# A second bank of inner products in a TensorE-bound mixer kernel: the third product of both mixers as seven half-size products over a VectorE base

## The chip, the cores and the metric

The kernel runs on one core of a Trainium2 chip. The metric is the device time of one execution in microseconds (us). All profiled runs named here are fast, with a mean granted TensorE clock between 0.995 and 1.0 of full speed. Ratios are the mean time of one kernel's fast runs over the mean of the other's from the same rounds, with a 95% interval. They are therefore not quite the ratio of the medians that are quoted next to them.

A profile's span is the time from the first to the last instruction of one execution. It is about 1.8 us shorter than the time of that execution (573.1 against 574.88 us before).

## The reference

```python
def reference(A_x, A_wqkv, A_wo, B_x, B_w1, B_b1, B_w2, B_b2):
    x = A_x                                             # 1 x 2048 x 1024
    h = x + attention(layernorm(x), A_wqkv, A_wo)       # linear attention, cut
    n = layernorm(layernorm(h))
    u = gelu(einsum("bsd,sf->bdf", n, w1) + b1)         # mixer 1: 2048 tokens -> 3584
    y = einsum("bdf,fs->bds", u, w2) + b2               # mixer 2: 3584 -> 2048
    return h + y.transpose(0, 2, 1)
```

The attention block takes the first 235 us and the change does not touch it. The two mixers are matrix products and take the rest.

## The kernel before

Both mixers are built from a seven-product scheme for 2 x 2 blocks (Strassen-Winograd), one "pair" of stationary tiles at a time. `p1` to `p7` are products of 512 columns, with 8 steps of the contraction in mixer 1 and 14 in mixer 2. Their results are combined in banks `A`, `B`, `C` of PSUM, the memory into which this program has TensorE write its results, and the fifth product goes to SBUF, where it keeps its working tiles, as `e`. `evac` is an eviction: it takes a finished result out of its bank.

```python
    def p1: mm(1, A);  ScalarE: B <- A
    def p6: mm(6, B);  ScalarE: C <- B       # both accumulate onto the copied bank
    def p2: mm(2, A);  evac(0, 0, A)
    def p7: mm(7, C);  evac_shared(1, C)     # VectorE: t = C + e, then out
    def p3: mm(3, B);  evac_shared(0, B)     # VectorE: t = B + e, then out
    def p4: mm(4, C);  evac(1, 0, C)
    def asum(m):  # VectorE: stationary operand of products 5, 6, 7, 3 as a sum of tiles
```

Two pairs form a "quad". One product of a quad, `m`, can itself be split by the same scheme: its four sub-blocks of 256 columns and half the contraction become seven inner products `i1` to `i7` instead of eight. A quad holds two pairs, so one product costs 16 matmuls of 512 columns in mixer 1; the seven inner products are 28 matmuls of 256 columns. (28 and 49 in mixer 2.)

```python
    class Inner:                              # a, e share one PSUM bank; b, c the other
        def i1: mm(1, a); ScalarE: b <- a
        def i6: mm(6, b); ScalarE: c <- b
        def i2: mm(2, a); sink(0, 0, a)       # hand the finished part on
        def i5: mm(5, e); ScalarE: es <- e
        def i7: mm(7, c); sink_sum(1, 1, c, es)   # VectorE adds es
        def i3: mm(3, b); sink_sum(0, 1, b, es)
        def i4: mm(4, c); sink(1, 0, c)
```

Between these steps `interleave` puts the matmuls of another product as filler, so that TensorE has work while ScalarE and VectorE hand banks on. Before the change, mixer 1 has the first and the fifth product inner in its six later quads, mixer 2 the fifth in its three later quads:

```python
        def run(self, pend, nxt, ...):        # one quad
            interleave(self.in1, [st.p4 for st in pend])
            nxt = nxt()                       # weights of the next quad
            interleave(self.in5, [st.p6 for st in self.sts])
            pre(5)                            # VectorE sums for the NEXT quad
            for st in self.sts: st.p2()
            pre(6)
            for st in self.sts: st.p7()
            pre(7)
            for st in self.sts: st.p3()
            pre(3)
```

In mixer 2, `out` takes a result through an SBUF tile `ot` (three of them) and writes it out with a DMA; `hr` are tiles of the residual `h`, read back from memory.

Of the kernel before, what the change touches and what calls it, by code (L numbers as in the profile page):

```python
# [8 lines left out]
P = 128  # L9
# [18 lines left out]
def kernel(  # L28
# [171 lines left out]
    class Inner:  # L200
        def __init__(self, sts, m, mov, tag, sink, sink_sum):
            self.nk, self.mov, self.tag = sts[0].nk // 2, mov, tag
            self.sink, self.sink_sum = sink, sink_sum
            L = [st.lhs[m].rearrange("p (k two) f -> p k two f", two=2) for st in sts]
            self.a11, self.a12, self.a21, self.a22 = (L[i][:, :, h, :] for i in range(2) for h in range(2))
            self.lhs = {1: self.a11, 2: self.a12, 4: self.a22}

        def sums(self):
            sm = [pools["is"].tile([P, self.nk, P], FP16, tag=self.tag, bufs=4, name="is")[:] for _ in range(4)]
            nc.vector.tensor_tensor(sm[0], self.a21, self.a22, ALU.add)  # L210
            nc.vector.tensor_tensor(sm[1], sm[0], self.a11, ALU.subtract)
            nc.vector.tensor_tensor(sm[2], self.a11, self.a21, ALU.subtract)
            nc.vector.tensor_tensor(sm[3], self.a12, sm[1], ALU.subtract)
            self.lhs.update({5: sm[0], 6: sm[1], 7: sm[2], 3: sm[3]})
# [23 lines left out]
        def i5(self):  # L238
            self.mm(5, self.e, True)
            self.es = cpool.tile([P, HW], F32, tag="es", name="es")  # L240
            nc.scalar.copy(self.es[:], self.e)

        def i7(self):
            self.mm(7, self.c, False)
            self.sink_sum(1, 1, self.c, self.es[:])

        def i3(self):
            self.mm(3, self.b, False)
            self.sink_sum(0, 1, self.b, self.es[:])
# [5 lines left out]
    class Product7:  # L255
# [9 lines left out]
        def prefetch(self):  # L265
            pass

        def asum(self, m):
            a, b, op = {
                5: (self.a21, self.a22, ALU.add),  # L270
                6: (self.lhs.get(5), self.a11, ALU.subtract),
                7: (self.a11, self.a21, ALU.subtract),
                3: (self.a12, self.lhs.get(6), ALU.subtract),
            }[m]
            t = pools["sa"].tile([P, self.nk, P], FP16, tag="sa", name="sa")[:]
            self.lhs[m] = t
            return nc.vector.tensor_tensor(t, a, b, op)  # L277
# [50 lines left out]
        def p7(self, cut=None):  # L328
            self.mm(7, self.C, False)
# [4 lines left out]
            self.evac_shared(1, self.C)  # L334
# [34 lines left out]
    class Mixer2(Product7):  # L369
        def __init__(self, p):  # L370
            super().__init__(p, w2_tiles[p], NFP, gmov)

        def prefetch(self):
            self.hr = {}
            for sh in range(2):
                for dh in range(2):
                    t = outp.tile([P, CW], BF16, tag=f"hr{self.p % 2}{sh}{dh}", bufs=2 if (sh, dh) == (1, 0) else 1, name="hr")
                    nc.sync.dma_start(t[:], h_dram[2 * self.p + sh][:, dh * CW:(dh + 1) * CW])
                    self.hr[sh, dh] = t

        def out(self, sh, dh, a, b, op):
            i = 2 * self.p + sh
            ot = outp.tile([P, CW], BF16, tag="ot", bufs=3, name="ot")
# [21 lines left out]

    class Quad:
        def __init__(self, sts, mov1, mov5):
            self.sts = sts
            self.mov1, self.mov5 = mov1, mov5
# [19 lines left out]

        def pre(self, m):  # L430
            if m == 5 and self.mov1 is not None:
                self.in1 = Inner(self.sts, 1, self.mov1, "i1", self.sink1, self.sum1)
                self.in1.sums()
            for st in self.sts:
                st.asum(m)
            if m == 5:
                self.in5 = Inner(self.sts, 5, self.mov5, "i5", self.sink5, self.sum5)
                self.in5.sums()

        def prefetch(self):  # L440
            for st in self.sts:
                st.prefetch()

        def run(self, pend, nxt, on_p4=nop, before_p7=nop, on_p7=nop, cut=None):
            nk = self.sts[0].nk

            def interleave(n, fs):
                steps = [(f, k) for f in fs for k in range(nk)]
                t = len(steps)
                cuts = [0, (5 * t + 8) // 16, (9 * t + 8) // 16, (12 * t + 8) // 16, t]  # L450

                def fill(q):
                    part = steps[cuts[q]:cuts[q + 1]]
                    for f in fs:
                        ks = [k for g, k in part if g is f]
                        if ks:
                            f(ks)

                for f in (n.i1, 0, n.i6, n.i2, 1, n.i5, n.i7, 2, n.i3, 3, n.i4):
                    fill(f) if isinstance(f, int) else f()  # L460

            if self.mov1 is not None:
                for st in self.sts:
                    st.begin()
                interleave(self.in1, [st.p4 for st in pend])
            else:
                for st in self.sts:
                    st.p1()
                for st in pend:
                    st.p4()  # L470
            on_p4()
            nxt = nxt()
            for st in self.sts:
                st.shared_tile()
            interleave(self.in5, [st.p6 for st in self.sts])
            pre = nxt.pre if nxt is not None else (lambda m: None)
            pre(5)
            for st in self.sts:
                st.p2()
            pre(6)  # L480
            before_p7()
            for st in self.sts:
                st.p7(cut if st is self.sts[-1] else None)
            on_p7()
            pre(7)
            for st in self.sts:
                st.p3()
            pre(3)
# [13 lines left out]

    def run_pair(st, pend, nxt, after1=nop, after5=nop, on_p4=nop, before_p7=nop, on_p7=nop):
        st.p1()
        after1()
        if not pend:
            h = st.nk // 2
            st.p5(list(range(st.nk - 1)))
            st.p2(list(range(h)))
            st.p5([st.nk - 1])  # L510
        else:
            for q in pend:
                q.p4()
            on_p4()
            st.p5()
        after5()
        nxt.pre(5)
        st.p6()
        nxt.pre(6)
        st.p2(None if pend else list(range(h, st.nk)))  # L520
        before_p7()
        st.p7()
        on_p7()
        nxt.pre(7)
        st.p3()
        nxt.pre(3)
        return [st]
# [662 lines left out]
    pools["is"] = inner1  # L1190
    hmov.update(moving(hE, hO, hT2, hT3, hT4))
    mov1, sums1 = inner_moving(hE[:, :, 0:CW], NSP, inner1, "hi1")
    mov5, sums5 = inner_moving(hE[:, :, CW:D], NSP, inner1, "hi5")
    NQ1 = NFP // 2

    def next_load1(u):
        def load():
            if u < NQ1:
                load_w1(u, 0)
                load_w1(u, 1)  # L1200
            else:
                load_w2(0, wpool)
        return load

    def quad1(u):
        return Quad([Mixer1(2 * u), Mixer1(2 * u + 1)], mov1, mov5)

    nxt = Mixer1(1)
    pend = run_pair(cur, [], nxt)
    cur, nxt = nxt, quad1(1)  # L1210

    pend = run_pair(cur, pend, nxt, after1=sums1, after5=sums5)
    for u in range(1, NQ1):
        cur = nxt
        pend, nxt = cur.run(pend, lambda: quad1(u + 1) if u + 1 < NQ1 else None, on_p4=next_load1(u + 1))
# [4 lines left out]
    pools["sa"] = ctx.enter_context(tc.tile_pool(name="sapool2", bufs=6, side="right", reuse_waits="tile"))  # L1220
# [4 lines left out]
    pools["is"] = inner2  # L1225
# [4 lines left out]
    cur.asum(5)  # L1230
    for sl in spans:
        nc.vector.tensor_tensor(gT2[:, sl, :], gO[:, sl, CW:D], gE[:, sl, CW:D], ALU.subtract)
    for m in (6, 7, 3):
        cur.asum(m)
# [15 lines left out]
    mov5, sums5 = inner_moving(gE[:, :, CW:D], NFP, inner2, "gi5")  # L1250

    def quad2(u):
        return Quad([Mixer2(2 * u), Mixer2(2 * u + 1)], None, mov5)

    def after_p4(u):
        def act():
# [4 lines left out]
        return act  # L1261

    pend = [cur, Mixer2(1)]
    nxt = quad2(1)
    for st in pend:
        st.prefetch()
        if st is pend[1]:
            for m in (5, 6, 7, 3):
                st.asum(m)
            make_t3()  # L1270
        st.p1()
        st.p5()
        st.p2()
        st.p6()
    sums5()
    nxt.pre(5)
    for st in pend:
        st.p7()
    make_t4()
    nxt.pre(6)  # L1280
    nxt.pre(7)
    for st in pend:
        st.p3()
    nxt.pre(3)
    for u in range(1, NSP // 2):
        cur = nxt
        cur.prefetch()
        last = 2 * u + 2 == NSP
        pend, nxt = cur.run(
            pend, lambda: None if last else quad2(u + 1),  # L1290
            on_p4=after_p4(u), on_p7=make_t4, cut=CW - P if last else None,
        )
# [32 lines left out]
```

## Time and profile before

| | before |
|---|---|
| time, median of 4 runs | 574.91 us (574.85 to 575.26) |
| TensorE (PE) | 566.0 us busy, 99% of the span |
| VectorE (DVE) | 383.8 us, 67% |
| ScalarE (ACT) | 254.7 us, 44% |
| DMA | 41.7% of the 16 engines' time on the main queue |

The page of the profile of before, parts 1 and 4. Part 1 gives busy time, share and number of instructions. Part 4 is the chain of work that ended last, followed back from the end, as shares of the span.

```profile
span 573.1 us, 8081 instructions
...
PE 566.0 (99%) x3061; PEld 287.2 (50%) x3061; DVE 383.8 (67%) x731; ACT 254.7 (44%) x547; POOL 1.8 (0%) x8
...
PE 93%; DVE 3%; DMA 2%; ACT 2%; issue 1%; SPq 0%; ACTq 0%
```

TensorE is busy for the whole span and the chain is TensorE. The busy share does not show small losses at hand-offs, so I also used a finer measure. From the trace's matmul starts, a matmul of 512 columns follows its predecessor after 0.216 us and one of 256 columns after 0.109 us (medians in the mixers). Everything by which a start comes later than this cadence I call *excess*. It is read for every pair of neighbouring matmuls and assigned to the place where it falls. Before the change the excess was 3.04 us in mixer 1 and none in mixer 2 (-0.09).

A quad of mixer 1: the timeline, where each line is start, duration, engine, source line, operation, output <- inputs, and in brackets how long the engine stood idle and what ended it. SPq is the queue from which SyncE issues the DMAs. `...` marks rows left out.

```profile
341.93 1.89 PE L285 MATMUL psA_3760<-hO,wq 128*128 128x512 f16 x8
...
343.42 0.42 DVE L210 TENSOR_TENSOR is<-wq 128x512 f16<-128x512 bf16 x1 [2.16 <-DMA wq<-in_B_w_dram]
343.65 1.89 PE L285 MATMUL psA_3762<-hO,wq 128*128 128x512 f16 x8
...
345.38 1.89 PE L285 MATMUL psC_3856<-hT_2231,sa 128*128 128x512 f16 x8
```

VectorE stood 2.16 us at the head of its queue, waiting for the next quad's weights, and TensorE went on with `p2` and `p7` without a gap (1.89 us of busy time for 8 matmuls, starts 1.72 us apart). Second, the end of the kernel:

```profile
569.47 0.62 DVE L388 SCALAR_TENSOR_TENSOR ot<-psC_5541,b_sb,hr 128x384 bf16<-128x384 f32 x1 [1.52 <-PE psC_5541 L285]
569.65 0.55 PE L285 MATMUL psC_5618<-gs_5626,wq 128*128 128x128 f16 x7
570.25 0.35 DVE L388 SCALAR_TENSOR_TENSOR ot<-psC_5618,b_sb,hr 128x128 bf16<-128x128 f32 x1 [0.16 <-PE psC_5618 L285]
```

The last two evictions follow TensorE directly. From the start of the last matmul to the end of the span it is 3.1 us.

### The profile page before, as it was taken

What the parts mean: (1) busy time and instruction counts of PE and PEld (TensorE: products, weight loads), DVE (VectorE), ACT (ScalarE), POOL (GpSimd) and SP (SyncE); (2) the same over time, 40 slices, a digit from 0 to 9 for tenths busy, and PEclk for the clock granted to TensorE, in tenths of its full rate; (3) what the DMA queues carried; (4) which work ended last, traced back from release to release, by engine and by line L of the source; (5) the groups of instructions that cost most, each with busy time, mean ns of one, the idle gap of its engine ahead of it and who ended that gap; (6) DMA issues with size and microseconds to landing.
All of it is one profiled execution on the core that took longest, in us unless ns stands there. A gap on an engine that the chain in (4) does not pass through costs nothing.

```text
span 573.1 us, 8081 instructions
## 1 busy us (share of the span) xinstructions
PE 566.0 (99%) x3061; PEld 287.2 (50%) x3061; DVE 383.8 (67%) x731; ACT 254.7 (44%) x547; POOL 1.8 (0%) x8
## 2 busy tenths in 40 slices
PE   8999999999999999999999999999999999999997
PEld 3444444455555444446555565564444554544544
DVE  6898887556767879863745727442989558557535
ACT  5657777656667776445445354463110100100100
POOL 1000000000000000000000000000000000000000
PEclk9999999999999999999999999999999999999999
DMA  9934432039536762104041240425971852842001
GB/s 309 352 74 83 85 73 38 19 113 318 104 73 130 184 174 102 55 2 146 1 148 55 93 148 1 148 75 146 233 189 47 218 140 67 218 120 73 19 27 47
DMA packets 97798, 66.59 MB, mean 116 GB/s; under 512 B 32082, under 2 KB 91744, under 8 KB 97760
## 3 DMA queue, kind: packets, MB, share of 16 engines
q1 hardware_dynamic: 97024, 65.42, 41.7%
q10 hardware_dynamic: 672, 0.66, 0.3%
q8 instruction: 24, 0.39, 0.3%
q14 instruction: 14, 0.11, 0.1%
q0 software_dynamic: 64, 0.01, 0.0%
HBM read 50.34 MB, written 8.39 MB: 102 GB/s over the span
## 4 chain that ended last, share of the span: by engine, by line
PE 93%; DVE 3%; DMA 2%; ACT 2%; issue 1%; SPq 0%; ACTq 0%
PE acc_t L964 9%; PE acc_t L1112 9%; PE psB L695 4%; PE psC L695 4%; PE psA L695 4%; PE psE L695 2%; PE nd_ps L1063 1%; DMA xr<-in_A_x_dram 1%; PE psB_4758 L285 1%; PE psC_5500 L285 1%; PE psC_5181 L285 1%; PE psB_5064 L285 1%; PE psC_4858 L285 1%; PE psA_4757 L285 1%; PE psC_4527 L285 1%; PE psB_4550 L285 1%
## 5 line engine op out<-in xcount | busy, mean ns | idle before, releaser
L285 PEld LDWEIGHTS <-sa 128*128 128x128 f16 x716 | 70.0, 98 | 77.3 <-issue 0.7
L285 PEld LDWEIGHTS <-wq 128*128 128x128 bf16 x590 | 57.1, 98 | 61.7 <-issue 1.0
L964 PE MATMUL acc_t<-xnT,wq_sb 128*128 128x512 bf16 x256 | 58.0, 379 | 0.0
L1112 PE MATMUL acc_t<-wo_sb,pqT 128*128 128x512 bf16 x256 | 56.1, 379 | 0.0
L277 DVE TENSOR_TENSOR sa<-wq 128x1024 f16<-128x1024 bf16 (+1 forms) x44 | 36.4, 830 | 6.9 <-DMA wq<-in_B_w_dram 2.8
L1112 PEld LDWEIGHTS <-pqT 128*128 128x128 bf16 x256 | 24.8, 98 | 29.0
L964 PEld LDWEIGHTS <-wq_sb 128*128 128x128 bf16 x256 | 24.5, 98 | 27.4
L166 ACT ACTIVATE e_sb<-acc_t 128x512 bf16<-128x512 f32 x40 | 23.9, 597 | 26.5 <-PE acc_t L964 24.3
L170 DVE TENSOR_SCALAR e_sb<-e_sb 128x512 bf16<-128x512 bf16 x64 | 18.5, 289 | 25.4 <-ACT e_sb L166 24.8
L218 PEld LDWEIGHTS <-is 128*128 128x128 f16 x276 | 26.9, 98 | 14.3 <-issue 3.0
L695 PEld LDWEIGHTS <-xs 128*128 128x128 f16 x208 | 20.0, 98 | 23.3 <-DVE xs L681 1.3
L695 PE MATMUL psA<-wkv,xnT 128*128 128x512 bf16 x104 | 26.7, 379 | 0.0
L1123 DVE BATCH_NORM_STATS2 hst<-acc_t 128x6 f32<-128x512 f32 x32 | 22.1, 693 | 6.7 <-ACT h_bf L1122 6.5
L1110 ACT CAST acc_t<-xr 128x512 f32<-128x512 bf16 x32 | 19.0, 593 | 13.4 <-DVE hst L1123 13.3
L695 PEld LDWEIGHTS <-xnT 128*128 128x128 bf16 x156 | 15.3, 98 | 18.5 <-issue 0.2
L167 ACT ACTIVATE r_sb<-acc_t 128x512 bf16<-128x512 f32 x40 | 23.7, 593 | 0.0
L619 PE MATMUL acc_t<-wkv,xnT 128*128 128x512 bf16 x96 | 21.6, 379 | 0.7 <-ACT xnT L872 0.7
L1084 DVE TENSOR_TENSOR o_sb<-nd_ps,rd 128x384 bf16<-128x384 f32 (+1 forms) x48 | 21.7, 504 | 0.6 <-ACT rd L1079 0.4
L588 DVE BATCH_NORM_STATS2 st<-x_sb 128x6 f32<-128x512 bf16 x32 | 20.5, 681 | 1.6 <-DMA x_sb<-in_A_x_dram 1.6
L277 DVE TENSOR_TENSOR sa<-sa,wq 128x1024 f16<-128x1024 f16 (+1 forms) x22 | 18.3, 831 | 3.9 <-PE psC_4858 L285 2.3
L277 DVE TENSOR_TENSOR sa<-wq,sa 128x1024 f16<-128x1024 bf16 (+1 forms) x22 | 18.3, 831 | 3.7 <-PE psI_5141 L218 1.1
L1122 ACT CAST h_bf<-acc_t 128x512 bf16<-128x512 f32 x32 | 18.4, 575 | 1.0 <-PE acc_t L1112 0.9
(722 smaller groups left out, 979.1 us busy)
## 6 DMA issues: line engine op xcount, KB each, us to landing
wq<-in_B_w_dram SPq DMA_DIRECT2D x14, 1024.0 KB, 7.7
wq<-in_B_w_dram SPq DMA_DIRECT2D x8, 1792.0 KB, 10.0
xr<-in_A_x_dram SPq DMA_DIRECT2D x16, 256.0 KB, 3.1
out_dram<-ot SPq DMA_DIRECT2D x31, 128.0 KB, 1.7
x_sb<-in_A_x_dram SPq DMA_DIRECT2D x15, 256.0 KB, 3.2
wkv<-in_A_wqkv_dram SPq DMA_DIRECT2D x2, 1024.0 KB, 9.5
wq_sb<-in_A_wqkv_dram SPq DMA_DIRECT2D x2, 1024.0 KB, 12.7
wo_sb<-in_A_wo_dram SPq DMA_DIRECT2D x2, 1024.0 KB, 6.4
```

The costliest lines, as they stand in the source:

```text
L166: pin(nc.scalar.activation(e_sb[:], src, ACT.Exp))
L167: pin(nc.scalar.activation(r_sb[:], src, ACT.Relu))
L218: nc.tensor.matmul(ps, lhsT=self.lhs[m][:, k, :], rhs=self.mov[m][:, k, :], start=(start and k == 0), stop=(k == self.nk - 1), skip_group_ ...
L277: return nc.vector.tensor_tensor(t, a, b, op)
L285: nc.tensor.matmul(ps[:, cols], lhsT=lhs[:, k, :], rhs=mv(k)[:, cols], start=(start and k == 0), stop=(k == self.nk - 1), skip_group_check ...
L588: return nc.vector.bn_stats(st[:, c, :], x_sb[:, c * CW:(c + 1) * CW])
L619: mm = nc.tensor.matmul(pp[:, 0:CW], lhsT=xnT[:, kt, i * P:(i + 1) * P], rhs=wkv[:, kt, c * CW:(c + 1) * CW], start=(kt == 0), stop=(kt == ...
L695: pin(nc.tensor.matmul(ps[:], lhsT=lhs[:, k, :], rhs=rhs[:, k, :], start=(start and k == 0), stop=(k == hk2 - 1), skip_group_check=True,))
L964: nc.tensor.matmul(qp[:, 0:SW], lhsT=wq_sb[:, kt, j * P:(j + 1) * P], rhs=xnT[:, kt, u * SW:(u + 1) * SW], start=(kt == 0), stop=(kt == ND ...
L1084: nc.vector.tensor_tensor(o_sb[:, b * JPB * P:(b * JPB + nsl) * P].rearrange("p (s h e) -> p s h e", h=HB, e=DH), blk[:, :, 0:P].rearrange ...
L1112: nc.tensor.matmul(ap_[:, 0:CW], lhsT=pqT[:, j, i * P:(i + 1) * P], rhs=wo_sb[:, j, dc * CW:(dc + 1) * CW], start=(j == 0 and not SEED_RES ...
L1123: nc.vector.bn_stats(st[:, dc, :], ap_[:, 0:CW])
```

## The change

The intent is to spare TensorE more columns. The third product becomes inner in all later quads of both mixers, and the fifth also in the first quads. `B` of the third product can't be a bank that the inner products accumulate on, because the inner results are parts of it; so VectorE builds a base `T = B + e` in SBUF and adds the inner results to it. To make room in SBUF, some sums are written in place and some rings of tiles are smaller. The core of the diff, cut:

```diff
@@ class Inner
         def i5(self):
             self.mm(5, self.e, True)
-            self.es = cpool.tile([P, HW], F32, tag="es", name="es")
-            nc.scalar.copy(self.es[:], self.e)
+            if self.mid is not None:
+                self.mid(self.e)                    # third product: VectorE, into T
+            else:
+                ... as before, in a shared tile
@@ class Product7, asum
-            t = pools["sa"].tile([P, self.nk, P], FP16, tag="sa", name="sa")[:]
+            if m == 3 and self.in_place:            # mixer 2
+                t = self.lhs[6]
+            elif m == 7:
+                t = self.a21.bitcast(FP16)          # over the weights
+            else:
+                t = pools["sa"].tile([P, self.nk, P], FP16, tag="sa", name="sa")[:]
@@ class Mixer2, out
-            ot = outp.tile([P, CW], BF16, tag="ot", bufs=3, name="ot")
+            ot = outp.tile([P, CW], BF16, tag="ot", bufs=2, name="ot")
@@ class Quad
+        def base3(self):                            # T = B + e, once for each pair
+                nc.vector.tensor_tensor(t[:], st.B[:], st.e[:], ALU.add)
+        def mid3(self, e):                          # inner fifth product into both T
+                nc.vector.tensor_tensor(t[:, HW:CW], e, t[:, HW:CW], ALU.add)
+        def sum3(self, m, h, ps, es=None):          # the other inner results
+            nc.vector.tensor_tensor(t[:, c], ps, t[:, c], ALU.add)
+            if (m, h) in ((0, 1), (1, 0)):
+                self.sts[m].evac(0, 1, t)
@@ Quad.run
+            self.pre(6)                             # own sums, not the next quad's
+            self.pre(7)
             interleave(self.in5, [st.p6 for st in self.sts])
-            pre(5); p2; pre(6); p7; pre(7); p3; pre(3)      (shortened)
+            self.base3()
+            self.pre(3)
+            self.each("p2")
+            interleave(self.in3, self.p7s(), self.nk)
+            self.tail(nxt)                          # prefetch, then nxt.pre(5)
```

Not shown: a new routine `first` for the first quads, the residual tiles `hr` in one ring of four, and one dummy matmul that seeds a bank.

## The prediction

> **What bounds the kernel now.** TensorE. The profile's first part has PE busy 566.0 of 573.1 us (99%), granted clock 1.0; the chain of waits is 93% PE. From the trace's matmul starts, a 512-column matmul issues every 0.216 us and a 256-column one every 0.109 us[...]. Over both mixers (230 us to the end) everything beyond this cadence sums to about 3 us, 1.4 of it in the first 6 us of mixer 1. VectorE is 67% busy, ScalarE 44%. So only fewer PE columns can help, and any new wait shows in full.
>
> **What PE is spared.** One product of a quad costs 16 (mixer 1) or 28 (mixer 2) matmuls of 512, as seven inner products 28 or 49 of 256: 3.46 -> 3.05 us and 6.05 -> 5.34 us. Seven such replacements in mixer 1 (third product in six quads, fifth in the first) and four in mixer 2 save 7 x 0.40 + 4 x 0.71 = 5.7 us; one added seeding matmul costs 0.2. The reordered first quad should hide about 1 us of mixer 1's start-up waits. With no new waits: about 568.5 us.
>
> **What it adds.** VectorE per steady quad: four inner sums (0.42 us each in mixer 1, 0.62 in mixer 2), two 512-wide bases (0.69), two 256-wide adds and four sums (0.42), less two shared evictions: about +4 us on about 14 of 23 us. The third product's chain passes through VectorE: its inner i5 waits for the first sum[...], i3 for the sum after two base adds, i4 for the next. [...] In the built order of mixer 1 ten operations for the next quad (about 5 us at the spacings in the timeline, 0.34 and 0.60 us) stand ahead of the first sum, behind a weight load that landed 1.5 us after the fifth product's end before; p2 and the first inner steps give PE about 6.7 us. My reckoning: i5 waits 0.4 us, i3 0.2, and ScalarE copies with little filler (i6, i7 of the next first product, p6) another 0.5: roughly 1 us per mixer 1 quad against 0.2 before, which eats more than the 0.40 saved. Mixer 2 has longer fillers: 0.3 us per quad, but about 1 us in its first quad, where VectorE has a solid 22 us queue before the fifth product's second sum.
>
> **Sum.** Savings 5.4 + 1; new waits 3 to 8 us, central 5.5. I predict 574.0 us, 570.0 to 578.0. Faster by over 2% 0.01 (fewer columns cannot give it), within 2% 0.97, slower 0.02.
>
> **What would show each step.** PE matmul count +169 and column time 5.5 us less; 256-column cadence still 0.109. PE gaps in the timeline before inner i5 and i3 of the third product, with VectorE as releaser, about 0.4 and 0.2 us in each mixer 1 quad and nearly none in mixer 2's later quads; ScalarE-released gaps before i6, i7 and p6. VectorE busy up by about 30 us.
>
> **What would make it wrong.** If VectorE reaches the first sum earlier (weight load lands sooner, as PE's own waits give it time), mixer 1's waits vanish: 569 to 570. If waits on output buffers (two, not three) cascade in mixer 2, 578 or more.

The marked cuts take out what was said of the hardware without a trace or run of this case that shows it; no term of the sum is among them. Its 5.4 + 1 of savings less 5.5 of new waits are 0.9 us off the 574.9 of before, the 574.0 predicted.

## The result, and the profile after

| | before | after |
|---|---|---|
| median | 574.91 us | 582.70 us (582.12 to 583.42, 4 runs) |
| ratio | | 1.0135 [1.0117, 1.0152] |
| PE busy | 566.0 us, 3061 matmuls | 565.1 us, 3230 matmuls |
| DVE busy | 383.8 us | 425.6 us |
| ACT busy | 254.7 us | 261.3 us |
| excess in mixer 1 | 3.04 us | 10.35 us |
| excess in mixer 2 | -0.09 us | 4.75 us |
| start of last matmul to the end | 3.1 us | 5.1 us |

The change made the kernel slower by 7.8 us, 1.35%, and outside the range of the prediction. The profiled execution of after was the slowest of its four (583.42 us; the fastest took 582.12), so its waits lie at the upper end. Parts 1 and 4 of the page after:

```profile
span 581.6 us, 8567 instructions
...
PE 565.1 (97%) x3230; PEld 303.9 (52%) x3230; DVE 425.6 (73%) x841; ACT 261.3 (45%) x571; POOL 1.8 (0%) x8
...
PE 18%; DMA 4%; DVE 3%; issue 1%; DVEq 0%
```

The chain could be followed only through the last 26% of the span, which is why PE has only 18%. What is telling is the mix within it: DMA and DVE have 7 of those 26 points, where before the chain was nearly all PE. By the lines of the same part, 3 of DMA's 4 points are loads of weights, which are not bigger than they were.

The difference of the two spans is 8.5 us and adds up. The column time of the replaced products falls by 7 x 0.40 + 4 x 0.71 - 0.2 = 5.4 us, worked out from the two cadences, which did not change. The excess of both mixers rises from 2.95 to 15.10, by 12.15 us, and the end of the kernel grows by 2.0. -5.4 + 12.15 + 2.0 is 8.7. The other 0.2 us are a gain at the start: the first matmul of the mixers, which is the added dummy, starts at 235.15 us and not at 235.35. The saving came, and waits took it and more.

**Mixer 1, third product.** Here is the third of the five quads that have it with weights for a next quad (timeline of after). In after, `L288` is the sum `asum`, `L210` the sums of an inner product, `L473` the addition of an inner result to the base `T`.

```profile
321.22 0.42 DVE L210 TENSOR_TENSOR is<-wq 128x512 f16<-128x512 bf16 x1 [1.21 <-DMA wq<-in_B_w_dram]
...
324.45 1.03 PE L296 MATMUL psC<-hT,wq 128*128 128x512 f16 x4
324.97 1.29 DVE L288 TENSOR_TENSOR wq<-wq 128x1024 f16<-128x1024 bf16 x2
326.18 0.42 DVE L210 TENSOR_TENSOR is<-sa 128x512 f16<-128x512 f16 x1
326.51 0.42 DVE L473 TENSOR_TENSOR tb<-psI,tb 128x256 f32<-128x256 f32 x1
...
326.99 0.60 PE L218 MATMUL psI<-hO,is 128*128 128x256 f16 x4 [1.51 <-DVE tb L473]
```

TensorE's inner `i5` at 326.99 waited for the first `L473`, which the bracket names as its releaser. (In the program `i5` writes `e`, and that addition reads `a`, the other half of the same bank. That the shared bank is why it waits was not tested by a run.) That addition takes 0.42 us. Its input was ready soon after 324.45, where the matmuls that make it give way to the filler. But ahead of it in VectorE's queue stood ten sums for the *next* quad and one more sum, from 321.22 to 326.5, and the first of those stood 1.21 us waiting for weights. The excess there is 1.67 us (my measure; the profile's 1.51 models the end of a matmul a little later). Compare the fifth of these quads, in the same execution, where the weights came in time:

```profile
370.96 0.42 DVE L210 TENSOR_TENSOR is<-wq 128x512 f16<-128x512 bf16 x1
...
376.24 0.42 DVE L473 TENSOR_TENSOR tb<-psI,tb 128x256 f32<-128x256 f32 x1
...
376.72 0.49 PE L218 MATMUL psI<-hO,is 128*128 128x256 f16 x3 [0.21 <-DVE tb L473]
```

The queue alone, without waiting for a load, leaves a wait of 0.37 us (0.21 in the profile's measure). In the five quads (the sixth and last has no next quad and no wait) the excess before `i5` was 0.81, 0.37, 1.67, 1.59 and 0.37 us, and VectorE's idle time for the weights 0.35, none, 1.21, 1.13 and none. The landing of a load of the same size at the same place in the program differs by over a microsecond within one execution: the second weight load of each of these quads took 8.1, 8.0, 9.4, 9.2 and 7.8 us from issue to landing. Why it varies is open. Before the change it took 7.7 to 7.8 us each time, and VectorE's waits for it, 1.05 to 2.17 us, cost nothing.

**Mixer 2, fifth product.** A quad of mixer 2, timeline of after; `L458` adds an inner result of the fifth product to `e`.

```profile
462.51 0.93 PE L218 MATMUL psI<-gE,is 128*128 128x256 f16 x7
462.59 1.09 DVE L288 TENSOR_TENSOR sa<-wq 128x1792 f16<-128x1792 bf16 x1 [2.51 <-DMA wq<-in_B_w_dram]
...
465.73 0.42 DVE L458 TENSOR_TENSOR e<-psI,es 128x256 f32<-128x256 f32 x1
466.19 0.92 PE L218 MATMUL psI<-gE,is 128*128 128x256 f16 x7 [0.92 <-DVE e L458]
```

It is the same shape: a sum for the next quad stands at the head of VectorE's queue for 2.51 us, waits for its weights, and behind it stands the addition that TensorE needs. The load had been issued at 453.94, 8.6 us before VectorE could go on. The excess was 1.08 us in this quad, 1.78 in the next, 0 in the last, which has no next quad; the first quad lost 1.24 us before `i6` of its fifth product. There a sum at 429.65 released it (1.08 us in the profile's measure), and VectorE had worked without a gap of over 0.04 us since 405.57.

**The end.** Timeline of after; `L403` is the eviction into an output tile.

```profile
570.70 6.03 PE L296 MATMUL psC<-gs,wq 128*128 128x512 f16 x41
...
574.35 0.75 DVE L403 SCALAR_TENSOR_TENSOR ot<-tb,b_sb,hr 128x512 bf16<-128x512 f32 x1 [0.27 <-DMA out_dram<-ot]
576.15 1.42 DVE L403 SCALAR_TENSOR_TENSOR ot<-psC,b_sb,hr 128x512 bf16<-128x512 f32 x2 [1.05 <-DMA out_dram<-ot]
578.79 0.35 DVE L403 SCALAR_TENSOR_TENSOR ot<-psC,b_sb,hr 128x128 bf16<-128x128 f32 x1 [1.22 <-DMA out_dram<-ot]
```

The last evictions now wait for the writes of earlier results (a write of 128 KB takes 1.7 us from issue to landing, median), and there are two output tiles and not three. Two tiles alone are not the cause: e6_no3 below also has two output tiles, but a plain third product, and its end takes 3.1 us as before. There the four evictions before the last start at 566.68, 569.11, 571.35 and 573.62 us; with the inner third product they are crowded at 571.74, 573.39, 574.35 and 576.15.

**Small waits on ScalarE in mixer 1**, from five quads each: 0.31 us before `p6`, 0.17 before `i7` and 0.09 before `i6` of the first product; and 0.15 before the third product's `i3`, which waits on VectorE. Together 0.72 us a quad, 3.6 us.

### The profile page after: what moved, and what is told of

It is laid out like the page before. It is cut to its first block, busy times and chain, and to the rows that moved or that the text cites. A ratio compares the mean times of both kernels' runs of the same rounds, so it can differ in the third digit from the quotient of the medians.

```text
span 581.6 us, 8567 instructions
## 1 busy us (share of the span) xinstructions
PE 565.1 (97%) x3230; PEld 303.9 (52%) x3230; DVE 425.6 (73%) x841; ACT 261.3 (45%) x571; POOL 1.8 (0%) x8
## 5 line engine op out<-in xcount | busy, mean ns | idle before, releaser
L296 PEld LDWEIGHTS <-wq 128*128 128x128 bf16 (+1 forms) x814 | 79.1, 98 | 79.0 <-issue 1.1
L218 PEld LDWEIGHTS <-is 128*128 128x128 f16 x500 | 48.5, 97 | 33.8 <-issue 14.1
L296 PE MATMUL psC<-hT,wq 128*128 128x512 f16 x224 | 56.2, 379 | 0.0
L296 PE MATMUL psC<-gs,wq 128*128 128x512 f16 (+2 forms) x238 | 51.6, 366 | 0.0
L296 PEld LDWEIGHTS <-sa 128*128 128x128 f16 x268 | 26.2, 98 | 25.0 <-issue 1.6
L218 PEld LDWEIGHTS <-sa 128*128 128x128 f16 x303 | 29.6, 98 | 11.8 <-issue 0.6
L458 DVE TENSOR_TENSOR e<-psI,es 128x256 f32<-128x256 f32 x22 | 9.3, 424 | 35.7 <-PE psI L218 35.7
L332 ACT COPY psC<-psB 128x512 f32<-128x512 f32 x22 | 12.5, 570 | 45.4 <-PE psB L296 45.4
L296 PE MATMUL psB<-hT,sa 128*128 128x512 f16 x112 | 28.2, 379 | 0.7
L296 PE MATMUL psB<-gT,sa 128*128 128x512 f16 x112 | 26.5, 379 | 0.0
L296 PE MATMUL psA<-gE,wq 128*128 128x512 f16 x112 | 25.3, 379 | 0.0
L296 PE MATMUL psA<-hO,wq 128*128 128x512 f16 x112 | 25.3, 379 | 0.0
```

The source lines that it names most:

```text
L218: nc.tensor.matmul(ps, lhsT=self.lhs[m][:, k, :], rhs=self.mov[m][:, k, :], start=(start and k == 0), stop=(k == self.nk - 1), skip_group_ ...
L296: nc.tensor.matmul(ps[:, cols], lhsT=lhs[:, k, :], rhs=mv(k)[:, cols], start=(start and k == 0), stop=(k == self.nk - 1), skip_group_check ...
L332: nc.scalar.copy(self.C[:], self.B[:])
L458: nc.vector.tensor_tensor(self.sts[m].e[:, self.cols(h)], ps, es, ALU.add)
```

## The experiments

**The theory.** Three waits took the gain: (1) VectorE's queue in mixer 1, where sums for the next quad, with a wait for weights, stand ahead of the additions for `i5`; (2) the same in mixer 2; (3) at the end, evictions that wait for one of two output tiles. **Rivals.** (R1) The third product as such does not pay: its longer chain of hand-offs over VectorE costs more than the columns that it saves, whatever the order. (R2) The waits are only a symptom; VectorE has too much work (73%), and moving sums moves the waits. (R3) It is not the third product, but the new order of the program around it.

To reorder, I added to single instructions an order dependency without a semaphore. It makes the build place an instruction behind another on the same engine's queue, and leaves waits and data as they are:

```python
    def behind(ins, key):          # "schedule ins after marks[key]"; no semaphore
        if key in marks:
            tc.add_manual_dep(ins.ins, marks[key].ins.name, NoSync, reason="behind")
        return ins
```

All kernels gave correct results. The first four ran on one chip with each other and with before (574.93 us), the next four on a second (575.10), the last two on a third (574.93).

### e1_tail: the end alone

```diff
-            ot = outp.tile([P, CW], BF16, tag="ot", bufs=2, name="ot")
+            last = self.p >= NSP - 2
+            ot = self.hr[sh, dh] if last else outp.tile([P, CW], BF16, tag="ot", bufs=2, name="ot")
```

The last quad writes each result over its own residual tile, so no result waits for a free output tile. (Three output tiles as before did not fit: the build of after with three stops with the message that a pool needs 28 KB of a partition where 27.78 are left.)

> The changed kernel; only the last quad of mixer 2 writes its results over the residual tiles instead of into the two shared output tiles. Theory (the end of the changed kernel waits for the two output tiles to be written out): VectorE no longer waits for an output transfer after 574 us, the stretch from PE's last matmul to the end of the span falls from about 5 us to the 3.2 us of before, about 2 us less than the changed kernel (582.7 to about 580.7). Rival (VectorE has too much work in all, and runs late at the end because of that): the end stays where it is, within 0.5 us.

Measured: 580.54 us (580.22 to 582.65), ratio to before 1.0105 [1.0087, 1.0123], that is 2.2 us less than after. No eviction waits for an output write any more, but the end fell only to 3.9 us, not to the expected 3.1. The profiled execution is 3.0 us shorter than that of after: 1.2 us of it at the end, and 2.0 in mixer 1, which this edit leaves alone (excess 8.37 and not 10.35, with one late load and not two). So the repair is worth about 1.2 us, and the agreement with the expected 2 us is luck. Its timeline shows what is left at the end:

```profile
572.69 0.42 SPq L393 DMA_DIRECT2D hr<-h_dram  x1
...
575.00 0.88 DVE L404 SCALAR_TENSOR_TENSOR hr<-psC,b_sb,hr 128x384 bf16<-128x384 f32 x2 [1.41 <-PE psC L296]
```

The bracket names TensorE, but the matmuls of these 384 columns were done by about 574.2 us (an estimate: the matmuls after them start at 573.97, and in before this eviction starts 0.21 us after those). VectorE also waits for the last residual tile, whose load was issued at 572.69 and landed at 574.92, 0.08 us before the eviction starts. With results in the residual tiles, that load reuses a tile from which an earlier result is written out. Two such writes stand ahead of it in SyncE's queue, the first issued at 570.71, 1.98 us before it; in e4_all a write takes 1.9 us from issue to landing (median of four). That the load was issued so late because of such a write is an inference from these times. The repair changed one wait for another, shorter one.

### e2_order2: VectorE's order in mixer 2 alone

```diff
-            return nc.vector.tensor_tensor(t, a, b, op)
+            ins = nc.vector.tensor_tensor(t, a, b, op)
+            if m == 5 and self.in_place:           # mixer 2
+                behind(ins, "sum5")
+            return ins
```

The next quad's first sum, the one that waits for weights, is placed behind the last of the two additions to `e` (`marks["sum5"]`, set in `sum5` for the first pair, which comes second).

> The changed kernel; in mixer 2 the next quad's first difference sum (which waits for a weight load) may no longer stand ahead of the current quad's two sums of the fifth product on VectorE. Same work, other order. Theory (a late load at the head of VectorE's queue): PE's waits of 1.1 and 1.8 us before the inner i3 of the fifth product in quads 1 and 2 of mixer 2 vanish, 2.9 us less than the changed kernel (about 579.8). Rival (amount of VectorE work): no change, within 0.5 us, as the work is the same.

Measured: 577.34 us (577.19 to 577.84), ratio 1.0044 [1.0027, 1.0060], 5.4 us less than after, and better than I expected. The excess in mixer 2 fell from 4.75 to 0.51 us; the 1.24 us of the first quad went too, which I had not counted on. These 4.2 us are the edit's. In the profiled execution another 1.8 us are not: only one of mixer 1's loads came late, so mixer 1's excess was 8.54 us and not 10.35. The same place in mixer 2 in the timeline of this run (lines are numbered differently: `L472` is the addition to `e`, `L299` is `asum`):

```profile
461.12 0.42 DVE L472 TENSOR_TENSOR e<-psI,es 128x256 f32<-128x256 f32 x1 [0.94 <-PE psI L229]
...
461.93 0.93 PE L229 MATMUL psI<-gE,is 128*128 128x256 f16 x7
...
462.89 0.43 DVE L472 TENSOR_TENSOR e<-psI,es 128x256 f32<-128x256 f32 x1 [1.35 <-PE psI L229]
463.24 1.08 DVE L299 TENSOR_TENSOR sa<-wq 128x1792 f16<-128x1792 bf16 x1
```

The additions now wait for TensorE, and not the other way round; the sum follows behind both. VectorE does the same work, so R2 falls for mixer 2.

### e3_order1: VectorE's order in mixer 1 alone

```diff
+            if m == 6 and not self.in_place:       # mixer 1
+                behind(ins, "sum3")
...
-            nc.vector.tensor_tensor(t[:, c], ps, t[:, c], ALU.add)
+            ins = nc.vector.tensor_tensor(t[:, c], ps, t[:, c], ALU.add)
+            if (m, h) == (1, 0):
+                marks["sum3"] = ins
```

> The changed kernel; in mixer 1 two of the ten operations of the next quad that stand ahead of the first sum of the third product (its two sixth-product sums, 0.6 us each) are put behind the last sum of the third product. Same work, other order. Theory: the wait before inner i5 of the third product falls by up to 1.2 us in each of five quads: from 0.81, 0.37, 1.67, 1.59, 0.37 us to about 0, 0, 0.5, 0.4, 0 (the rest where the load lands late), so about 3.9 us less than the changed kernel (about 578.8). Rival (amount of VectorE work): within 0.5 us of the changed kernel.

Measured: 579.02 us (577.80 to 580.28), ratio 1.0071 [1.0050, 1.0092]. The excess in mixer 1 fell from 10.35 to 5.16 us, or from 8.4 to 8.5 if e1_tail and e2_order2 are taken, which like this run had one load about 1 us late. Of the waits before the third product's `i5` one of 0.27 us was left, in the quad where the load came 1.02 us late. In mixer 2, which this run leaves alone, the excess was 6.76 us instead of 4.75. From its timeline:

```profile
504.26 1.36 PE L229 MATMUL psI<-gE,is 128*128 128x256 f16 x7 [2.41 <-DVE e L472]
...
505.42 2.96 PE L310 MATMUL psB<-gT,sa 128*128 128x512 f16 x7
```

A wait of 2.58 us (my measure) was followed by a stretch at half the clock: the trace has a granted clock of 0.5 from 504.60 to 508.01 us, and 7 matmuls of 512 columns took 2.96 us there instead of 1.67. This stretch is 1.6 of the 2.0 us by which mixer 2 differs. Of the four runs two took 580.0 to 580.3 us with a mean clock of 0.995 and 0.996, the others 577.8 and 578.0 with 0.998. That the median meets the expectation is therefore partly luck; what the edit does is read from mixer 1 alone.

### e4_all: the three edits together

As above, with product 7's sum also behind in mixer 1.

> The three edits together, and in mixer 1 the two seventh-product sums put back as well (four of ten operations, 2.4 us). Theory: the savings add: 2.0 + 2.9 + 4.8 us less than the changed kernel, about 573.0, just below the kernel before (574.9); what is left over the ideal is 1.24 us in mixer 2's first quad and about 3 us of ScalarE-released waits in mixer 1. Rival: about 582.

Measured: 573.07 us (572.70 to 573.47), ratio 0.9968 [0.9953, 0.9982]. This is 9.6 us less than after and 1.9 less than before, so it beats both kernels. The excess was 5.1 us in mixer 1 and 0.5 in mixer 2. Against after's profiled execution that is 5.25 us less in mixer 1, 4.25 less in mixer 2 and 1.3 less at the end; I had counted on 4.8, 2.9 and 2.0, so the total was met better than its parts. The end of its timeline:

```profile
561.46 6.03 PE L312 MATMUL psC<-gs,wq 128*128 128x512 f16 x41
...
565.26 0.42 SPq L409 DMA_DIRECT2D hr<-h_dram  x1
...
567.47 0.88 DVE L420 SCALAR_TENSOR_TENSOR hr<-psC,b_sb,hr 128x384 bf16<-128x384 f32 x2 [1.30 <-PE psC L312]
```

The end takes 3.8 us, against 3.1 in before. As in e1_tail, the last evictions wait for the load of a residual tile, issued at 565.26 and landed at 567.39, and not only for TensorE, which the bracket names. R1 and R2 fall as explanations of the loss: the third product stays inner, VectorE is at 425.0 us as in after, and the loss is gone.

### e4_again: the same kernel, five rounds on another chip

> The kernel with the three repairs once more, for the comparison on the same chip: 573.0, 0.997 of the kernel before, as in the first run.

Measured: 572.96 us (572.58 to 575.72, 6 runs), ratio 0.9966 [0.9943, 0.9989]. One of its runs took 575.72 and one of before's 578.62; both widen the interval. The profiled execution is that slow one. Its delay lies before the mixers: their first matmul starts at 238.0 us and not at 235.4, and the trace has a clock of 0.5 from 8.6 to 12.0 us. The mixers are the same as in the first run to 0.05 us of excess (5.13 and 0.51). It holds the best test of the theory, because in two quads the weights came late again, by 1.42 and 1.07 us. In this numbering `L492` is the addition to `T`:

```profile
322.99 0.43 DVE L221 TENSOR_TENSOR is<-wq 128x512 f16<-128x512 bf16 x1 [1.42 <-DMA wq<-in_B_w_dram]
...
326.00 1.03 PE L312 MATMUL psC<-hT,wq 128*128 128x512 f16 x4
326.21 0.42 DVE L492 TENSOR_TENSOR tb<-psI,tb 128x256 f32<-128x256 f32 x1
...
326.87 0.60 PE L229 MATMUL psI<-hO,is 128*128 128x256 f16 x4
```

The load was later than in the worst quad of after (1.21), and TensorE's `i5` did not wait: four of the ten sums have moved away from in front of `L492`, which now starts 0.2 us into the filler rather than 2 us after its start. So the late load was only half of the cause. The length of the queue behind it was the other half, and it is the half that the program decides.

### e6_no3: the change without the third product

`base3`, `in3` and the third product's moving sums are left out, `p7` and `p3` are plain; everything else is as in after, without the repairs.

```diff
-            self.base3()
+            if 3 in self.movs: self.base3()          # 3 is not in movs here
...
-            interleave(self.in3, self.p7s(), self.nk)
-            self.tail(nxt)
+            for f in self.p7s(): f(None)
+            self.tail(nxt)
+            self.each("p3")
```

> The changed kernel with the third product as before (two plain products, shared evictions); the fifth product inner in the first quads, in-place sums and buffers as changed; no order edit. Theory (most of the loss comes with the third product's chain): 575 to 577 us, at least 5 us under the changed kernel: of the savings 1.1 and the start's 0.8 us stay, against about 2 us at the end and 1.5 us in mixer 2's first quad. Rival (the buffers, in-place sums and first quads lose the time): 581 or more.

Measured: 579.38 us (579.31 to 579.86), ratio 1.0077 [1.0062, 1.0092]. I missed this by over 2 us. Of the 7.8 us that the change costs, only 3.3 come with the third product. The other 4.3 come from the rest of it: 3.34 us of excess in mixer 2 against none (0.84 in the first quad, 1.19 and 0.91 in the two quads with a next one, which are the fifth product's, at the places where after has its waits), and 4.6 us of excess in mixer 1 against 3.04, less 0.9 us of columns. So R3 is half right. The end, where I had expected to lose 2 us, lost nothing:

```profile
568.12 6.24 PE L296 MATMUL psC<-gs,wq 128*128 128x512 f16 x42
...
574.40 0.35 DVE L403 SCALAR_TENSOR_TENSOR ot<-psC,b_sb,hr 128x128 bf16<-128x128 f32 x1 [0.16 <-PE psC L296]
```

From the last matmul's start to the end it is 3.1 us, with two output tiles (lines of e6_no3's timeline).

### e7_no3_fixed: the same with the repairs of the end and of mixer 2

> The same without the third product's seven inner products, with the end's edit and mixer 2's order edit. Theory: only the savings of the first quads remain, 574.9 less 0.9 less 0.8: about 573.0 us. Rival: as slow as the kernel before or slower.

Measured: 576.22 us (576.10 to 576.54), ratio 1.0021 [1.0006, 1.0036]. Another miss, by 3 us: I had expected it below before. The excess in mixer 2 is 0.27, so that repair works here too. But mixer 1 has 5.09 us: in each of five quads 0.15 to 0.33 us before the first product's `i6`, 0.35 and 0.20 before its later steps. The first two are released by ScalarE copies, the 0.20 by a VectorE sum that had itself waited for one. Before had two waits of 0.11 and 0.09 us a quad, apart from the first. In ScalarE's order the activations of the third product (0.72 us each) now stand ahead of the first product's copies. That the program's order causes these waits is an inference from the queue, since I ran no kernel that changes it alone.

Beside e4_all this gives the value of the third product: 573.07 with it, 576.22 without it, so it brings 3.1 us once the queues are in order. In the change as it was made, it cost 3.3 (582.70 against 579.38). The comparison with e4_all is between chips, each against 574.93 and 575.10 of before; e5_gelu, which differs from e4_all by one order edit and took the same time, ran on the chip of e7_no3_fixed with 572.95, 3.3 us less. In the profiled executions the third product saves 4.5 us of columns in e4_all and gives back 0.7 at the end and 0.2 of excess.

### e8_m2only: the third product inner in mixer 2 only

As e7_no3_fixed, with the inner third product and its base in mixer 2.

> As the last one, with the third product inner in mixer 2 only. Theory (there the fillers are long enough, once the queue is in order): three times 0.71 us less than the last one, about 570.9 us, and no PE wait over 0.15 us in mixer 2's quads 1 to 3. Rival (the third product's VectorE work costs as much as it saves): the same as the last one.

Measured: 575.41 us (574.76 to 576.13), ratio 1.0006 [0.9991, 1.0021]: 0.8 us less than e7_no3_fixed, not 2.1. From the first matmul of the mixers to the last it was 333.70 us against 335.89, that is 2.2 less, as expected, and no wait in mixer 2's later quads exceeds 0.12 us. The 2.2 us are shown in the stretch that the edit touches. In the profiled executions the mixers started 1.0 us later and the end took 0.8 us longer (3.9 against 3.1), so the spans differ by 0.4 us only. The start lies before anything that the edit touches. The end is part of the effect: as in e1_tail, the last evictions wait for a residual tile, which landed at 570.66, and e7_no3_fixed, with the same repair of the end but a plain third product, has no such wait.

### e5_gelu: ScalarE's order in mixer 1

With e4_all's edits, the activation of `p4`'s result is also placed behind the copy that `p6` waits for.

```diff
-            nc.scalar.activation(
+            ins = nc.scalar.activation(
...
+            if (fh, dh) == (1, 0):
+                behind(ins, "sum1")               # sum1: the copy B <- A, first pair
```

> The kernel of the three edits together (573.1 us), and in mixer 1 ScalarE's eviction of the fourth product may no longer stand ahead of the copy that the sixth product's first matmul waits for. Theory (order in ScalarE's queue, not its load): the five waits of 0.34 us before the sixth product fall to under 0.1, about 1.4 us less: 571.6 us. Rival (the chain sum, copy, matmul is itself too long): the waits stay, 573.

Measured: 572.95 us (572.67 to 573.26), ratio 0.9963 [0.9947, 0.9980]: the same as e4_all. The wait went, and came back a step later. The timelines of e4_again (first) and e5_gelu (second) at the same place; `psB<-hT,sa` are the matmuls of `p6`, `psI<-hi,is` at the end is `i6` of the fifth product:

```profile
312.98 0.69 ACT L385 ACTIVATE gO<-psC,b_sb 128x512 f16<-128x512 f32 x1 [0.94 <-PE psC L312]
...
313.57 0.38 ACT L469 COPY psB<-psA 128x256 f32<-128x256 f32 x1
...
313.99 1.24 PE L312 MATMUL psB<-hT,sa 128*128 128x512 f16 x5 [0.18 <-ACT psB L469]
```

```profile
310.41 0.36 ACT L471 COPY psB<-psA 128x256 f32<-128x256 f32 x1 [1.09 <-DVE psA L470]
...
310.68 0.69 ACT L385 ACTIVATE gO<-psC,b_sb 128x512 f16<-128x512 f32 x1
...
310.93 1.24 PE L312 MATMUL psB<-hT,sa 128*128 128x512 f16 x5
...
311.94 0.36 ACT L239 COPY psI<-psI 128x256 f32<-128x256 f32 x1
312.36 0.60 PE L229 MATMUL psI<-hi,is 128*128 128x256 f16 x4 [0.18 <-ACT psI L239]
```

With the activation moved behind the first copy, `p6` starts without a wait, but the activation now delays the copies of the next inner product. The excess before `p6` was 0.34 us five times, the excess before `i6` is 0.345 us five times. So it is not one misplaced instruction. My guess was that in this stretch ScalarE has several evictions with only about as much TensorE work beside them; e9_sumb tests it.

### e9_sumb: one ScalarE copy less

```diff
         def sum1(self, m, h, ps, es):
             nc.vector.tensor_tensor(A[:, c], ps, es, ALU.add)
-            nc.scalar.copy(B[:, c], A[:, c])
+            nc.vector.tensor_tensor(B[:, c], ps, es, ALU.add)      (placed first)
```

> The kernel with all three repairs, with the second half of the first sum (B) computed by VectorE directly from the bank and the base instead of by ScalarE copying the first half. Theory that ScalarE's queue is what is left in mixer 1: the wait of 0.34 us before the sixth product goes in five quads and does not come back elsewhere[...]; 1.2 to 1.7 us off, about 571.6. Rival: what is left is the length of the chain bank, sum, eviction, not ScalarE's load: the waits move to VectorE's side, time unchanged at 573.0.

Measured: 573.72 us (573.54 to 573.90), ratio 0.9971 [0.9949, 0.9994], beside 572.96 of e4_again on the same chip: not better, rather worse. The wait before `p6` is still 0.31 us in five quads, now right behind VectorE's sum, and a new one of 0.19 us stands before `i6` of the fifth product, so mixer 1's excess is 5.93 against 5.13. The timeline, where `L468` writes B:

```profile
310.33 0.42 DVE L221 TENSOR_TENSOR is<-sa 128x512 f16<-128x512 f16 x1
...
310.67 0.42 DVE L468 TENSOR_TENSOR psB<-psI,es 128x256 f32<-128x256 f32 x1
...
311.15 0.59 PE L312 MATMUL psB<-hT,sa 128*128 128x512 f16 x2
```

The copies that the edit takes from ScalarE took 0.36 to 0.38 us each (e4_again, `L469`). The sum again stands behind one that is needed later (`L221`, for this quad's third product). The build also moved filler: between the inner `i3` and `p6` stand one matmul of `p4` and four of the next `i1`, where e4_again has three of `p4`, four of `i4` and four of the next `i1`. So the experiment changed two things. ScalarE's load as the only cause is not supported. What sets mixer 1's last 5 us stays open.

## Why the prediction was wrong

Point by point, in the prediction's own steps:

- **"What bounds the kernel now": right.** TensorE bounds it, and new waits showed in full: column time, excess, end and start together account for the whole change.
- **"What PE is spared": right.** 169 more matmuls, unchanged cadences of 0.216 and 0.109 us, 5.4 us of columns saved, and about 0.8 us of start-up waits recovered in mixer 1 (1.36 to 0.61 us).
- **"i5 waits 0.4 us": the term was mis-sized.** 0.37 us is what it costs when the weights come in time. With the real landings the mean is 0.96 us in five quads, 4.8 us in all against the 2.0 predicted. I had read from before's trace that a load landed 1.5 us late and took that as a constant, which it nearly is in before (7.7 to 7.8 us from issue); in after it moves by over 1 us from quad to quad, and with the queue behind it the three late landings passed to TensorE: VectorE's idle times of 0.35, 1.21 and 1.13 us went with an excess of 0.44, 1.30 and 1.22 us over the 0.37 of the other two quads.
- **"i3 0.2" and "another 0.5" for ScalarE: right,** 0.15 and 0.57 us.
- **"about 1 us in its first quad" of mixer 2: right,** 1.24 us at the predicted place, with 0.4 beside it.
- **"Mixer 2 has longer fillers: 0.3 us per quad": the step that failed in its mechanism.** The fillers are longer, but I asked only how long VectorE's work is. The head of its queue was an instruction for the next quad that waited 2.5 us for a load. Measured 1.08, 1.78 and 0 us. e2_order2 takes all of it away without taking any work off VectorE.
- **Output buffers: named only as a risk** ("578 or more"), and left out of the central sum. It could be read from the diff: one output tile less. The end cost 2.0 us more, and e1_tail took 1.2 off it. But the tile alone is not the cause: e6_no3 has two tiles as well and loses nothing at the end. Evictions that the inner third product crowds together are needed too, and the prediction does not have them.

Summed: the excess rose by 12.15 us rather than by "3 to 8" of new waits less 1 at the start, and 2.0 at the end that weren't in the sum. Against the prediction's own terms the wait of `i5` was 2.8 us over, mixer 2's later quads 2.0, its first quad 0.7, the end 2.0. The two failures in VectorE's queue have one root: the queue was reckoned by its amount of work. What stands ahead was counted by its durations only, and it includes waits as well: in after's mixer 2 a 0.42 us addition, whose inputs were ready by about 464.2, stood behind sums of which the first had waited 2.51 us for a DMA, to 462.59. It started at 465.73, and TensorE lost 1.08 us, although the delayed matmul doesn't use that load.

The first expected runs without the third product (e6_no3, e7_no3_fixed) missed as well, in the same direction: I thought the rest of the change harmless, and its new order costs mixer 1 about 2 us (excess 5.09 against 3.04). The traces show most of these waits released by ScalarE copies; that ScalarE's order makes them is a guess, and the cause stays open.

## What to carry to other kernels

When a saturated engine gets a new dependence on another, don't ask how busy that one is (VectorE was as busy in e4_all as in after, 425.0 and 425.6 us), but which instructions stand ahead of the needed one in its queue, and whether one of them waits for a load; put work for later stages behind, not before. Here late loads cost nothing in before, where VectorE waited 1.05 to 2.17 us for them with nothing urgent behind; in after, with the addition for `i5` behind them, waits of 1.13 and 1.21 us went with 1.59 and 1.67 us of excess. And when a change gives up a buffer to fit, look at the end of the kernel, where no work was left to cover the wait (2.0 us here), and at what the new order puts there. Read a repair's worth from the stretch that it touches: here the whole time moved by 2 us with the landing of a few loads.
